# Routing constants later on GpSimd, one gate difference formed on TensorE, six warm-up products fewer

## The chip, the cores and the metric

The program runs on one core of a Trainium2 chip. A core has five engines that run their own instruction streams in order: TensorE (PE, with its weight loads shown as PEld), VectorE (DVE), ScalarE (ACT), GpSimd (POOL) and SyncE (SP), which here issues nearly all transfers. The metric is the device time of one execution in microseconds; lower is better.

## The reference

Three stages follow one another on 1536 tokens (2 batches, 8 heads, 768 steps, 40 columns a head, so 320 columns a token).

```
m_new = np.maximum(f_gate[:, :, t] + m, i_gate[:, :, t])
f_stab = np.exp(f_gate[:, :, t] + m - m_new)
i_stab = np.exp(i_gate[:, :, t] - m_new)
C = f_stab * C + i_stab * outer(v, k);  n = f_stab * n + i_stab * k
y[:, :, t] = sigmoid(o_gate) * (C q) / max(|n q|, 1)
...
h = x @ w_in;  g = softplus(h);  x = g @ w_out            # 320 -> 2048 -> 320
...
e_idx = np.argmax(x @ w_gate, axis=1)                      # one of 8 experts for each token
ye = np.maximum(x[mask] @ w1[e], 0.0) @ w2[e]              # 320 -> 1024 -> 320
out[mask] = gate_w * eom * ye
```

## The kernel before

The steps of the first stage are taken in six chunks of 128, for both batches, as products of 128x128 blocks. The names in the trace are those of the tiles. The gates of a chunk are prepared by `gates`: a scan gives `mm` (the running maximum m), `fg` becomes the decay, its cumulative sum is `acum`, and `ig` becomes i - m. Both `acum` and `ig` are turned by TensorE into one PSUM tile `gps`, and ScalarE takes their exponentials into `gts`. `gates` runs three times: for chunk 0, chunk 1, and chunks 2 to 5 together. Then, for a chunk and a batch: `sp` = k·q, `abc` = the decay between steps (for chunks 2 to 5 it is loaded from DRAM as a broadcast of `acum`, masked by an affine_select on GpSimd, and put through exponentials on ScalarE), `abc<-sp,abc` on VectorE, `pv` = scores times values, `qc` = carried state times q, and `kv`, the update of the carried state `cst`. `kv` reads `v<-v,sm`, which GpSimd makes. The output goes through `y`, is turned (`xp`), and split into a high part `win<-xp` and a low part `wou<-xp`.

The second stage's weights come in packed as `wra` in 16 pieces (a ring of three buffers). Each is converted by three VectorE instructions (`wta<-wra`), cast into a high part (`win<-wta` or `wou<-wta`, 128x704), and the low parts are subtractions: 128x576 on VectorE and 64x128 on GpSimd (function `low_p`). A round of `ph` (eight products) is one of the 16 pieces for one block of 256 tokens; there are 96 rounds. ScalarE makes `ab` of `ph` (three passes), VectorE makes `g`, ScalarE casts it to `gh`, VectorE subtracts for `gl`, and `acc` (six products) reads `gh` and `gl`.

The third stage first routes tokens. `constants` makes what routing needs: fifteen small GpSimd instructions (`tri`, `iota8`, `tokid`, `pad` and others), four loads of the gate weights `wg`, and 19 transfers that clear `rows` in DRAM from `pad`.

The order on the engines is made when the program is built. Each function is a task that yields the engine that it wants next ("P", "A", "V", "G", "S"); a planner (`Weaver`) with a price for each instruction picks the task that could start first by its own clocks, and by rank where they tie. A task that yields a number waits until so many rounds of `ph` have been planned. What is planned is fixed: each engine then runs its stream in order, and waits for semaphores. So a changed task changes the order of many others around it.

`heat` stands first on TensorE: products of a tile of ones that depend on no data. `W.clock["P"]` behind it tells the planner when TensorE is free.

Of the kernel before, what the change touches and what calls it, by code (L numbers as in the profile page):

```python
# [8 lines left out]
F32 = mybir.dt.float32  # L9
F32R = mybir.dt.float32r  # L10
BF16 = mybir.dt.bfloat16
# [3 lines left out]
ALU = mybir.AluOpType  # L15
# [4 lines left out]
RAWS = (2, 3, 3, 3, 3)  # L20
DRAM = bass.MemoryType.DRAM

HEAT = 50
EARLY = 4
P = 128
NEG = -1.0e30
# [208 lines left out]
def mlstm_moe_kernel(ctx: ExitStack, tc: tile.TileContext, q_t, k_t, k, v, i_gate, f_gate, o_gate,  # L235
                     w_in, w_gate, w_og, w1, w2, out):
    nc = tc.nc
    W = Weaver()
    PE, ACT, DVE, POOL, SP = (Priced(W, e, l) for e, l in
                              ((nc.tensor, "P"), (nc.scalar, "A"), (nc.vector, "V"), (nc.gpsimd, "G"), (nc.sync, "S")))  # L240
# [18 lines left out]
    NSP = 2  # L259
# [5 lines left out]
    G = B * H  # L265
# [11 lines left out]
    moe = moe_cm.__enter__()  # L277
# [28 lines left out]
    ig = moe.tile([GG, S], F32, tag="xl0", name="ig")  # L306
    mm = moe.tile([GG, S], F32, tag="row0", name="mm")
# [20 lines left out]
    def events(n, users=1):  # L328
# [15 lines left out]
    ident = const.tile([P, P], F32, name="ident")  # L344
    make_identity(nc, ident)
    identb = const.tile([P, P], BF16, name="identb")
    POOL.tensor_copy(out=identb, in_=ident)
    scratch_all = moe.tile([P, (3 + NSP) * P + P // 2], F32, tag="row2", name="scratch")
    after_t = scratch_all[:, (3 + NSP) * P:].bitcast(BF16)
    POOL.memset(after_t, 0.0)  # L350
    POOL.affine_select(out=after_t, in_=after_t, pattern=[[1, P]], compare_op=ALU.is_ge, fill=NEG, base=0,
                       channel_multiplier=-1)
    scratch = scratch_all[0:GG, 0:(3 + NSP) * P]
# [28 lines left out]
    def heat():  # L382
        warm, ev = yield from bank.get([P, 2 * P], F32, "heat")
        W.clock["P"] = 1.1
        yield "P"
        for _ in range(HEAT):
            PE.matmul(warm, ones, ones.unsqueeze(1).to_broadcast([P, 2, P]), start=True, stop=True)
        W.clock["P"] = 8.1
        W.signal(ev)

    def gates(n, c0, c1):
        yield [have_fi]
        t0, t1 = c0 * P, c1 * P
        p0 = max(t0, 1)
        if n:
            yield [gate_scan[n - 1], have_g[n - 1]]
        yield "V"
        DVE.tensor_tensor_scan(out=mm[:, t0:t1], data0=fg[:, t0:t1], data1=ig[:, t0:t1],
                               initial=NEG if n == 0 else mm[:, t0 - 1:t0], op0=ALU.add, op1=ALU.max)
        if n < 2:  # L400
            W.signal(gate_scan[n])
        yield "V"
        DVE.tensor_tensor(out=fg[:, p0:t1], in0=fg[:, p0:t1], in1=mm[:, p0 - 1:t1 - 1], op=ALU.add)
        yield "V"
        DVE.tensor_tensor(out=fg[:, p0:t1], in0=fg[:, p0:t1], in1=mm[:, p0:t1], op=ALU.subtract)
        yield "V"
        DVE.tensor_scalar(out=fg[:, p0:t1], in0=fg[:, p0:t1], scalar1=-104.0, scalar2=None, op0=ALU.max)
        if n == 0:
            DVE.memset(fg[:, 0:1], 0.0)
        yield "V"  # L410
        for c in range(c0, c1):
            cs = slice(c * P, (c + 1) * P)
            DVE.tensor_tensor_scan(out=acum[:, cs], data0=keep, data1=fg[:, cs], initial=0.0,
                                   op0=ALU.mult, op1=ALU.add)
        have_cum = Event(W.cur.out)
        for c in range(c0, min(c1, NSP)):
            a, p3 = acum[:, c * P:(c + 1) * P], parts3[:, c * P:(c + 1) * P]
            yield "V"
            DVE.tensor_copy(out=p3, in_=a)
            yield "V"  # L420
            DVE.tensor_tensor(out=rest, in0=a, in1=p3, op=ALU.subtract)
            yield "V"
            DVE.tensor_copy(out=p3[32:64], in_=rest[32:64])
            DVE.tensor_copy(out=second[64:GG], in_=rest[64:GG])
            yield "V"
            DVE.tensor_tensor(out=p3[64:GG], in0=rest[64:GG], in1=second[64:GG], op=ALU.subtract)
            have_acum[c].t = W.cur.out
        W.add(store_a(max(c0, NSP), c1, have_cum), 0)
        yield "V"
        DVE.tensor_tensor(out=ig[:, t0:t1], in0=ig[:, t0:t1], in1=mm[:, t0:t1], op=ALU.subtract)  # L430
        gps, gev = yield from bank.get([P, 2, NCH, G], F32, "gps")
        yield "P"
        for c in range(c0, c1):
            PE.transpose(gps[:, 0, c, :], acum[0:G, c * P:(c + 1) * P], ident[:G, :G])
            PE.transpose(gps[:, 1, c, :], ig[0:G, c * P:(c + 1) * P], ident[:G, :G])
        cs = slice(c0, c1)
        yield "A"
        ACT.activation(out=eB[:, cs], in_=gps[:, 1, cs], func=AF.Exp)
        ACT.activation(out=eA[:, cs], in_=gps[:, 0, cs], func=AF.Exp)
        yield "V"  # L440
        DVE.tensor_scalar(out=nA[:, cs], in0=gps[:, 0, cs], scalar1=-1.0, scalar2=None, op0=ALU.mult)
        W.signal(gev)
        for c in range(c0, c1):
            W.signal(have_g[c])
        W.signal(have_gates)
        W.signal(read_acum)
        W.signal(read_parts)
# [3 lines left out]
    def store_a(c0, c1, ready):  # L451
        if c1 <= c0:
            return
        yield [ready, sent_w]
        yield "S"
        SP.dma_start(abc_dram[:, c0 * P:c1 * P], acum[0:G, c0 * P:c1 * P])
        have_ab = Event(W.cur.out)
        yield from loads_a(c0, c1, have_ab)
# [374 lines left out]
    base = const.tile([P, E], F32, name="base")  # L833
# [4 lines left out]
    have_const, have_rows = Event(), Event()  # L838

    def constants():  # L840
        yield 2.0
        yield "G"
        POOL.memset(tri, 1.0)
        POOL.affine_select(out=tri, in_=tri, pattern=[[1, P]], compare_op=ALU.is_gt, fill=0.0,
                           base=0, channel_multiplier=-1)
        POOL.iota(iota8, pattern=[[1, E]], base=0, channel_multiplier=0, allow_small_or_imprecise_dtypes=True)
        POOL.iota(tokid, pattern=[[P, NCH], [S, B]], base=0, channel_multiplier=1, allow_small_or_imprecise_dtypes=True)
        POOL.memset(pad, 0.0)
        POOL.memset(wg[64:P, 2], 0.0)
        POOL.memset(pad[:, CCOL + 1:CCOL + 2], BIG)  # L850
        for t in (room, nxt, s128, esl, base, newp, more_p):
            POOL.memset(t, 0.0)
        POOL.iota(rem, pattern=[[0, 1]], base=0, channel_multiplier=1, allow_small_or_imprecise_dtypes=True)
        yield "S"
        for j, w in enumerate((w_gate, w_og)):
            SP.dma_start(wg[:, 0:2, j * E:(j + 1) * E], w[0:256].rearrange("(a p) e -> p a e", p=P))
            SP.dma_start(wg[0:64, 2, j * E:(j + 1) * E], w[256:DM])
        W.signal(have_const)
        yield 12.0
        for s in range(SLOTS):  # L860
            yield "S"
            SP.dma_start(rows[s * P:(s + 1) * P, :], pad)
        W.signal(have_rows)
# [545 lines left out]
    def low_w2(qn, e, r, ev):  # L1409
# [3 lines left out]
        W.signal(w2_ready[qn])  # L1413

    W.add(heat(), 0)
    W.add(load_gates(), 0)
    W.add(early_a(), 0)
    W.add(gates(0, 0, 1), 0)
    W.add(gates(1, 1, 2), 0.5)
    W.add(gates(2, 2, NCH), 1)  # L1420
    W.add(loads(0, 1), 1)
    W.add(load_w(), 2)
# [4 lines left out]
    for c in range(NCH):  # L1427
        for b in range(B):
            W.add(chunk(b, c), 0 if c == 0 else 1.5 if c == 1 else 2 + 0.1 * c)
    W.add(constants(), 5)  # L1430
    up_t, down_t = Task(up1(), 2.0), Task(down1(), 2.0)
    W.tasks += [down_t, up_t]
# [226 lines left out]
    if SLOTS > NS:  # L1659
        used = nc.values_load(meta[0:1, P:P + 1], min_val=0, max_val=SLOTS * P)  # L1660
        with tc.tile_pool(name="rest", bufs=1) as xp_, tc.tile_pool(name="ps3", bufs=2, space=PSUM) as ps3, \
                ExitStack() as deeper:
            for s in range(NS, SLOTS):
# [32 lines left out]
                for j in range(F // P):  # L1696
# [4 lines left out]
                    out=out, out_offset=bass.IndirectOffsetOnAxis(ap=tkr, axis=0), in_=yr, in_offset=None,  # L1701
# [72 lines left out]
```

## Time and profile before

| what | us |
|---|---|
| median of 3 runs | 435.1 (434.52 to 436.67) |
| profiled execution, device time | 435.17 |
| its span in the trace | 433.5 |
| TensorE busy | 410.1 (95% of the span) |
| VectorE busy | 343.5 (79%) |
| ScalarE busy | 302.5 (70%) |
| GpSimd busy | 181.0 (42%) |

The span runs from the first to the last traced instruction; the device time has 1.67 us more around it. Busy shares are means over stretches with different limits.

### The profile page before, as it was taken

How to read it: one execution, taken by the hardware profiler on the slowest of the kernel's cores; microseconds unless marked ns; L12 is line 12 of the kernel's file. 1: busy time of each engine (PE TensorE's matmuls, PEld its weight loads, DVE VectorE, ACT ScalarE, POOL GpSimd, SP SyncE). 2: the span in 40 equal slices, each digit the busy share in tenths (PEclk: the TensorE clock that was granted, in tenths of full speed). 3: DMA queues.
4: the chain of work that ended last, by engine and by line, in shares of the span. 5: the costliest groups of instructions: out<-in, count | busy, mean ns of one | idle time of the engine just before them, and what ended most of it. 6: DMA issues, size and time to landing. Idle time of an engine off the chain costs nothing. (4 is left out here: it accounts for less than half of the span.)

```text
span 433.5 us, 9833 instructions
## 1 busy us (share of the span) xinstructions
PE 410.1 (95%) x3078; PEld 390.5 (90%) x3078; DVE 343.5 (79%) x904; ACT 302.5 (70%) x879; POOL 181.0 (42%) x246
## 2 busy tenths in 40 slices
PE   8877999999899999999999999899999999999994
PEld 6767999999899999999999999767998998998893
DVE  4999798998999999997657675666755898798663
ACT  2776699996868877777769669466798666566230
POOL 4256756756120111120201102127676287387654
PEclk9999899999999999999999999989999999999998
DMA  8958789499226412032101100128645636544112
GB/s 263 312 175 247 240 240 300 136 332 297 77 102 252 170 69 67 33 91 62 38 2 38 38 2 37 38 102 271 228 132 185 220 132 216 189 144 139 42 67 80
DMA packets 32284, 62.90 MB, mean 145 GB/s; under 512 B 4218, under 2 KB 16765, under 8 KB 32230
## 3 DMA queue, kind: packets, MB, share of 16 engines
q1 hardware_dynamic: 30742, 57.87, 41.0%
q0 software_dynamic: 1488, 4.35, 2.7%
q8 instruction: 28, 0.46, 0.4%
q14 instruction: 26, 0.21, 0.2%
HBM read 54.05 MB, written 8.65 MB: 145 GB/s over the span
## 5 line engine op out<-in xcount | busy, mean ns | idle before, releaser
L196 ACT ACTIVATE ab<-ab 128x256 f32<-128x256 f32 x192 | 77.4, 416 | 2.8
L196 PE MATMUL ph<-w1s,flat 128*128 x312 | 58.8, 332 | 2.6 <-DVE hr L196 1.5
L196 POOL TENSOR_TENSOR w1s<-w1raw,w1s 64x256 fp32r<-64x256 f32 (+1 forms) x39 | 39.4, 1027 | 48.5 <-ACT w1s L196 25.0
L196 PE MATMUL acc<-win,gh 128*128 128x320 f32 x240 | 56.1, 320 | 0.0
L196 DVE SCALAR_TENSOR_TENSOR g<-ph,ab 128x256 f32<-128x256 f32 x96 | 39.9, 419 | 20.2 <-ACT ab L196 19.5
L196 PE MATMUL yp<-w2s,hh 128*128 x240 | 54.6, 315 | 1.0 <-POOL w2s L196 0.9
L196 ACT ACTIVATE ab<-ph 128x256 f32<-128x256 f32 x96 | 36.0, 379 | 26.4 <-PE ph L196 26.2
L196 PEld LDWEIGHTS ph<-w1s,flat 128*128 128x128 f32 x312 | 46.6, 189 | 7.9 <-DVE hr L196 1.9
L196 DVE TENSOR_TENSOR gl<-g,gh 128x256 fp32r<-128x256 f32 x96 | 42.5, 447 | 7.9 <-ACT gh L196 7.2
L196 POOL DMA_INDIRECT rows<-row,rsm x12 | 12.0, 1004 | 80.4 <-DVE rsm L196 47.6
L196 POOL TENSOR_TENSOR w2s<-w2raw,w2s 128x640 fp32r<-128x640 f32 x22 | 39.1, 1808 | 8.7 <-issue 4.9
L196 ACT CAST gh<-g 128x256 fp32r<-128x256 f32 x96 | 38.1, 398 | 6.6 <-DVE g L196 4.7
L196 PEld LDWEIGHTS yp<-w2s,hh 128*128 128x128 f32 x240 | 39.8, 188 | 3.1 <-POOL w2s L196 1.1
L196 PE MATMUL ph<-win 128*128 128x256 f32 x250 | 40.8, 286 | 0.0
L196 DVE TENSOR_TENSOR hr<-ph,hr 128x256 f32<-128x256 f32 x60 | 24.7, 420 | 20.3 <-ACT hr L196 17.2
L196 PEld LDWEIGHTS acc<-win,gh 128*128 128x128 f32 x240 | 39.4, 191 | 0.0
L196 ACT COPY hr<-ph 128x256 f32<-128x256 f32 x60 | 22.6, 376 | 21.3 <-PE ph L196 19.2
L196 PE MATMUL acc<-win,gl 128*128 128x320 f32 x120 | 37.4, 312 | 0.0
L196 PE MATMUL yp<-w2s,hl 128*128 x120 | 37.2, 310 | 0.0
L196 PEld LDWEIGHTS ph<-win 128*128 128x128 f32 x250 | 34.3, 190 | 0.0
L196 PE MATMUL acc<-wou,gh 128*128 128x320 f32 x144 | 33.1, 315 | 1.2 <-ACT gh L196 1.2
L196 ACT CAST w2s<-w2raw 128x640 fp32r<-128x640 f32 x32 | 22.6, 735 | 13.9 <-PE yp L196 13.9
(209 smaller groups left out, 1070.6 us busy)
## 6 DMA issues: line engine op xcount, KB each, us to landing
w1raw<-in_w_dram SPq DMA_DIRECT2D x32, 384.0 KB, 4.4
wra<-in_w_in_dram SPq DMA_DIRECT2D x16, 704.0 KB, 5.1
w2raw<-in_w_dram SPq DMA_DIRECT2D x32, 320.0 KB, 3.2
abc<-abc_dram SPq DMA_DIRECT2D x4, 1024.0 KB, 7.8
rows<-pad SPq DMA_DIRECT2D x19, 194.0 KB, 4.4
qT<-in_q_t_dram SPq DMA_DIRECT2D x6, 512.0 KB, 4.4
kn<-in_k_dram SPq DMA_DIRECT2D x5, 416.0 KB
vn<-in_v_dram SPq DMA_DIRECT2D x6, 320.0 KB, 5.6
```

What stands on the lines that cost most here:

```text
L196: return fn(*args, **kw)
```

## The change

Four edits. The loop `heat` makes 44 products and not 50, and the planner is told 7.8 and not 8.1 for its end. In `gates` the VectorE subtraction `ig - mm` goes; in its place TensorE accumulates, behind the turned `ig`, a product of `mm` with a 16x16 tile `minus` (-1 on the diagonal), so that `gps` holds i - m. The tile `minus` is made by a memset and an affine_select on GpSimd at the start. `constants` waits for 20 planned rounds of `ph` before the GpSimd part (was 2), and for 26 before the clearing of `rows` (was 12).

```diff
-HEAT = 50
+HEAT = 44
...
-    scratch_all = moe.tile([P, (3 + NSP) * P + P // 2], F32, tag="row2", name="scratch")
-    after_t = scratch_all[:, (3 + NSP) * P:].bitcast(BF16)
+    scratch_all = moe.tile([P, (3 + NSP) * P + P // 2 + G], F32, tag="row2", name="scratch")
+    minus = scratch_all[0:G, (3 + NSP) * P + P // 2:]
+    POOL.memset(minus, 0.0)
+    POOL.affine_select(out=minus, in_=minus, pattern=[[-1, G]], compare_op=ALU.not_equal, fill=-1.0, base=0,
+                       channel_multiplier=1)
+    after_t = scratch_all[:, (3 + NSP) * P:(3 + NSP) * P + P // 2].bitcast(BF16)
...
-        W.clock["P"] = 8.1
+        W.clock["P"] = 7.8
...
-        yield "V"
-        DVE.tensor_tensor(out=ig[:, t0:t1], in0=ig[:, t0:t1], in1=mm[:, t0:t1], op=ALU.subtract)
...
-            PE.transpose(gps[:, 1, c, :], ig[0:G, c * P:(c + 1) * P], ident[:G, :G])
+            PE.matmul(gps[:, 1, c, :], ig[0:G, c * P:(c + 1) * P], ident[:G, :G], start=True, stop=False, is_transpose=True)
+            PE.matmul(gps[:, 1, c, :], mm[0:G, c * P:(c + 1) * P], minus, start=False, stop=True)
...
     def constants():
-        yield 2.0
+        yield 20.0
         yield "G"
...
-        yield 12.0
+        yield 26.0
         for s in range(SLOTS):
             yield "S"
             SP.dma_start(rows[s * P:(s + 1) * P, :], pad)
```

The change moves much more than these lines, since the planner runs anew. From the last routing step on, the order on all engines is the same as before (on TensorE the last 1581 rows of the program's order).

**GpSimd, at the update of chunk 1.** Before, with `v_575` the operand of `kv` for batch 1, in front of it the constants, in front of these `cst` of the same update:

```order
L196 TENSOR_TENSOR cst_111<-cst_111,sm 40x4x41 x2
L196 MEMSET tri 128x128
L196 AFFINE_SELECT tri<-tri 128x128
L196 IOTA iota_115 128x8
L196 IOTA tokid 128x12
L196 MEMSET pad 128x388
...
L196 IOTA rem 128x1
L196 TENSOR_TENSOR v_575<-v_378,sm 128x328
L196 TENSOR_TENSOR win<-wta,win 64x128
L196 AFFINE_SELECT abc<-abc 128x4x128
```

Now, where `v_584` is the same operand:

```order
L196 TENSOR_TENSOR cst_115<-cst_115,sm 40x4x41 x2
L196 TENSOR_TENSOR win<-wta,win 64x128
L196 TENSOR_TENSOR v_584<-v_374,sm 128x328
L196 AFFINE_SELECT abc<-abc 128x4x128 x2
L196 TENSOR_TENSOR v_608<-vn_83,gts 128x8x40
```

The constants are gone from here, and the low part of a weight piece stands ahead of the operand, where it stood behind.

**TensorE, behind the first two rounds of `ph`.** Before (`acc_560` and `acc_561` are the first sums of block 0):

```order
L196 MATMUL ph<-wou,win 128x256 x3
L196 MATMUL pv<-v_378,abc 128x123 x6
L196 MATMUL pv<-v_378,abc 128x82
L196 MATMUL pv<-v_378,abc 128x41
L196 MATMUL kv<-v_575,kn_85 104x82 x4
L196 MATMUL acc_560<-win,gh 128x320 x2
```

Now:

```order
L196 MATMUL ph<-wou,win 128x256 x3
L196 MATMUL kv<-v_584,kn_85 104x82 x4
L196 MATMUL sp<-qT_81,kT 128x128 x4
L196 MATMUL acc_569<-win,gh 128x320 x2
L196 MATMUL acc_569<-win,gl 128x320
L196 MATMUL acc_570<-win,gh 128x320 x2
L196 MATMUL acc_570<-win,gl 128x320
L196 MATMUL pv<-v_374,abc 128x123 x6
```

`kv` now follows `ph` at once, one `sp` of chunk 2 stands ahead of the first `acc`, and `pv` behind it.

**ScalarE, at the same place.** Before, with `sm<-abc` the first instruction that reads the loaded and masked `abc` of chunk 2:

```order
L196 CAST win<-wta 128x704
L196 ACTIVATE ab<-ph 128x256 x2
L196 ACTIVATE ab<-ab 128x256 x4
L196 CAST gh<-g 128x256
L196 CAST win<-wta 128x704
L196 CAST gh<-g 128x256
L196 ACTIVATE sm<-abc 128x4
```

Now:

```order
L196 CAST win<-wta 128x704
L196 ACTIVATE y<-y 128x320
L196 ACTIVATE ab<-ph 128x256
L196 ACTIVATE ab<-ab 128x256 x2
L196 ACTIVATE ab<-ph 128x256
L196 ACTIVATE ab<-ab 128x256
L196 ACTIVATE sm<-abc 128x4
L196 ACTIVATE abc<-abc,gts 128x128 x2
L196 ACTIVATE ab<-ab 128x256
L196 CAST gh<-g 128x256
```

The read of the loaded `abc`, which stood behind both `gh`, now stands ahead of the first. On SyncE the clearing transfers `rows<-pad`, which stood as 14 and 5 between loads of chunks 4 and 5 (the last load of `og` behind them), now stand as 12 and 7 behind all loads of the first stage.

## Rows read from the trace of the kernel before

**Rows 1.** Busy time by stretch: us, each engine (instructions), granted clock, DMA share, GB/s.
```profile
9.04:37.22 28.18, 23.67 (x211) 21.25 (x211) 27.24 (x54) 19.09 (x74) 11.15 (x17) 1.00 0.72 247
...
60.00:275.00 215.00, 213.00 (x1710) 211.40 (x1709) 181.41 (x526) 170.59 (x527) 55.47 (x82) 1.00 0.34 112
```

**Rows 2.** The same for the products of ones alone (TensorE).
```profile
1.14:6.00 4.86, 4.86 (x23) 1.00 0.83 210
6.00:9.04 3.04, 3.04 (x29) 1.00 1.01 350
```

**Rows 3.** Timeline of the start, all engines: start us, duration us.
```profile
4.28 2.46 SPq L196 DMA_DIRECT2D wra<-in_w_in_dram  x3
...
8.34 0.29 DVE L196 TENSOR_TENSOR ig<-ig,mm 80x128 f32<-80x128 f32 x1
...
9.13 0.21 PE L196 MATMUL gps<-ident,ig 16*128 16x16 f32 x1
...
12.66 0.52 DVE L196 TENSOR_SCALAR wta<-wra 128x704 uint32<-128x704 uint32 x1
```

**Rows 4.** Transfers issued 4.9 to 5.3: KB, median us to landing.
```profile
wra<-in_w_in_dram SPq DMA_DIRECT2D x1, 704.0 KB, 9.6
```

**Rows 5.** Timeline of VectorE, 30 to 75.
```profile
31.24 0.67 DVE L196 TENSOR_TENSOR ig<-ig,mm 80x512 f32<-80x512 f32 x1
...
37.45 0.87 DVE L196 SCALAR_TENSOR_TENSOR wta<-wra,wta 128x704 uint32<-128x704 uint32 x1
```

**Rows 6.** Timeline of TensorE, 29 to 60; in brackets idle time before, and what ended it.
```profile
37.22 0.84 PE L196 MATMUL ph<-win 128*128 128x256 f32 x5
...
39.21 1.87 PE L196 MATMUL pv<-v,abc 128*128 128x123 f32 x16
43.26 1.47 PE L196 MATMUL kv<-v,kn 128*104 128x82 f32 x8 [2.17 <-POOL v L196]
...
54.91 1.16 PE L196 MATMUL sp<-qT,kT 104*128 104x128 f32 x8 [1.11 <-DVE abc L196]
```

**Rows 7.** Busy time by stretch, columns as in rows 1.
```profile
28.96:31.37 2.41, 0.52 (x4) 0.31 (x4) 2.41 (x5) 2.07 (x8) 1.34 (x3) 1.00 0.01 1
43.00:44.00 1.00, 0.74 (x6) 0.75 (x6) 1.00 (x2) 0.34 (x2) 0.85 (x3) 0.76 0.98 363
44.00:47.00 3.00, 3.00 (x16) 3.00 (x15) 2.84 (x9) 2.23 (x9) 2.53 (x5) 0.51 1.05 344
```

**Rows 8.** Timeline of GpSimd, 39 to 44.
```profile
39.27 0.66 POOL L196 MEMSET tri<- 128x128 bf16 x1
...
42.46 0.74 POOL L196 TENSOR_TENSOR v<-v,sm 128x328 f32<-128x328 f32 x1
43.28 0.58 POOL L196 TENSOR_TENSOR win<-wta,win 64x128 fp32r<-64x128 f32 x1
43.94 0.70 POOL L196 TENSOR_SCALAR_AFFINE_SELECT abc<-abc 128x512 f32<-128x512 f32 x1
```

**Rows 9.** Timeline of ScalarE, 38 to 47.
```profile
38.73 0.77 ACT L196 CAST win<-wta 128x704 fp32r<-128x704 f32 x1
...
41.46 0.41 ACT L196 CAST gh<-g 128x256 fp32r<-128x256 f32 x1 [0.19 <-DVE g L196]
...
44.91 1.28 ACT L196 ACTIVATE abc<-abc,gts 128x128 f32<-128x128 f32 x4
```

**Rows 10.** Timeline of SyncE's issues, 10 to 140.
```profile
34.36 0.39 SPq L196 DMA_DIRECT2D abc<-abc_dram  x1
...
90.18 8.79 SPq L196 DMA_DIRECT2D rows<-pad  x14
```

**Rows 11.** Transfers issued 34 to 34.7: KB, median us to landing.
```profile
abc<-abc_dram SPq DMA_DIRECT2D x1, 1024.0 KB, 8.2
```

**Rows 12.** Timeline, all engines, 103 to 117.
```profile
107.65 0.47 ACT L196 ACTIVATE y<-og 128x320 f32<-128x320 f32 x1 [1.36 <-DMA og<-in_o_gate_dram]
...
109.59 0.71 PE L196 MATMUL sp<-qT,kT 104*128 104x128 f32 x4 [0.55 <-DVE cst L196]
```

## Prediction, made before the changed kernel ran

> **What bounds the kernel now.** I read the busy time by stretch first. TensorE is the bound for most of the run: from 60 to 275 us it is busy 213.0 of 215 us [rows 1]. Whatever makes that stretch begin earlier shortens the run by as much, and whatever loads the other engines there costs nothing until TensorE waits. Ahead of it the picture is another. Between the products of ones and the first `ph` (9.04 to 37.22) TensorE is busy 23.67 of 28.18 us and VectorE 27.24 [rows 1]: VectorE runs without a gap, so work taken from it there comes off the time. Next I read the timeline of TensorE for its waits. The longest in the whole run is 2.17 us ahead of `kv` at 43.26, released by GpSimd's `v` [rows 6]. Behind it the granted clock falls: 0.76 from 43 to 44 and 0.51 from 44 to 47, the lower of its two levels (1.2 against 2.4 GHz), and 1.00 on either side [rows 7]. The time that this costs is 0.24 + 3 x 0.49 = 1.7 us, at the most, since the first row begins in the wait. So one place has cost 3.9 us. GpSimd's timeline says why it is late: `v` ran at 42.46, behind the constants that began at 39.27 [rows 8]. One more wait is near, 1.11 us ahead of `sp` at 54.91 [rows 6].
>
> **The change part by part.**
>
> *Six products of ones.* Their pace is not even: 23 in the first 4.86 us, 29 in the last 3.04 us [rows 2] (0.21 and 0.105 us each), though the granted clock reads 1.00 in both. The six come off the fast end: 0.63 us, so that `gps` can start at 8.4 and not at 9.04.
>
> *The subtraction on VectorE.* Three instructions go: 0.29 us for chunk 0 [rows 3], as much for chunk 1 (the same shape), 0.67 us for chunks 2 to 5 [rows 5]. The six products that replace them cost 0.21 us or less each [rows 3], overlap their neighbours, and stand in stretches in which TensorE has spare time (4.5 us of 28.18 [rows 1]): nothing. If that cover were gone they would cost at most 6 x 0.21 = 1.3 us. The two instructions for `minus` come on GpSimd at the start, which the trace doesn't show in this size; the nearest row is a memset of 128x128 with 0.66 us beside other work [rows 8], so 0 to 1.3 us, and I take nothing, since GpSimd's next operand waits for later loads.
>
> *What the earlier start is worth.* VectorE would reach its first conversion instruction 0.9 us earlier (0.29 + 0.63). It can't start it: three `wra` are issued in 2.46 us from 4.28 [rows 3], so the second at about 5.1, and that one lands 9.6 us later [rows 4], at 14.7. At the 350 GB/s of that stretch [rows 2] 704 KB take 2.1 us, so the first lands at about 12.6. Before, the instruction ran at 12.66 [rows 3]. The head start is spent waiting there, and nothing is left of it. Of the subtractions the two later ones remain, 0.28 + 0.67 = 0.95 us in a gapless stretch. So the first `ph` starts **1.0 us earlier**, at 36.2. Lower bound 0.6 (the order of VectorE's conversions is new, too), upper 1.9 (the load lands early enough after all).
>
> *The constants.* Now the place of the 2.17 us wait, followed in the new order. Two rounds of `ph` take 2.0 us (37.22 to 39.21 [rows 6]) and end at 38.2. `kv` stands next and needs `v`, which GpSimd runs behind `win`, and that waits for ScalarE's cast of the third weight piece. The conversion ended at 38.32 (37.45 + 0.87 [rows 5]), 1.0 earlier is 37.3; cast 0.77 [rows 9], `win` 0.58, `v` 0.74 [rows 8]: 39.4. **TensorE waits 1.2 us.** Then `kv` and one `sp`: half of 1.47 us (that row lies in the low clock) and 0.9 of 1.16 [rows 6], to 41.0. `acc` needs `gh`, and ScalarE now makes `gh` behind its first read of the masked `abc`. That load was issued at 34.36 [rows 10], gated by VectorE's `y`; the subtractions and one `wou` no longer stand ahead of this `y`, so some 1.5 us earlier, at 32.9. It took 8.2 us [rows 11]: landed at 41.1. GpSimd's mask 0.70 [rows 8], then on ScalarE a small read (0.2), two of four exponentials (half of 1.28), one `ab` (0.4, as `gh`) and `gh` 0.41 [rows 9]: 43.5. **TensorE waits 2.5 us more.** So the waits here are 3.7 us where they were 2.17 + 1.11 = 3.3; the later 1.11 I take as gone, since `sp` has eight heads in a row there now and the product on VectorE that frees its bank stands ahead. The waits give back −0.4 us; the constants' 3.2 us are off the path, but a load takes their place.
>
> What decides is the clock. If it stays high, 1.7 us come back. In the trace a wait of 2.17 us in one piece was followed by the low clock; a stretch of 2.41 us with only 0.52 us of work, in two waits, was not: its clock stayed 1.00 [rows 7]. The new waits are in two pieces with 1.6 us of work between them, which is nearer to the second, so I take the clock as high: **+1.7 − 0.4 = 1.3 us**. Both ends stay in the range. The Trainium skill (TensorE: Matmul & The Clock Gate, "HAM oscillation — how this bites in real kernels") says that a matmul stream broken by waits restarts at the lower rate and pays for it each time. The trace shows both, a wait with that end and two without it. By the rule the sum would lose the 1.7 us: that is the second case below.
>
> *The constants and the clearing, where they go.* The constants land at a place where GpSimd is idle three quarters of the time (55.47 us busy of 215 [rows 1]): nothing, or at worst their 3.2 us once more. The 14 clearing transfers stood at 90.18 for 8.79 us [rows 10] ahead of loads that the first stage wants. ScalarE then waited 1.36 us for `og`, and TensorE 0.55 us at 109.59 [rows 12], for a VectorE product behind ScalarE's chain. Now no load of that stage is behind them: **0.55 us**. At least 0; at most 1.4, if all of ScalarE's wait came through.
>
> **Sum:** 1.0 + 1.3 + 0.55 = 2.85 us off 435.17, the time of the profiled execution: **432.3 us**. The median, 435.1, is as good as the same. Behind the last routing step the order is unchanged, so nothing is gained or lost there.
>
> **The rivals.**
> B, *the clock falls again*: the wait of 2.5 us is longer than the 2.17 that was followed by the low clock. It costs 1.7 us: 434.0.
> C, *the waits close*: the first weight piece lands early (0.9 us more), and the load of `abc` too, so that only a third of the 3.7 us is left (2.5 more); with the 0.55 the sum is 6.2 us: 429.0. For it: 4.5 us of TensorE's idle time lie ahead of 37 us. Against: both loads are placed by rows.
> D, *slower*: ScalarE's stream waits in order. `ab`, `gh`, the next casts and with them `acc` are behind the read of `abc`; each us that the load lands behind 41.1 costs one, and the clock is then low. It ends on the slow side from a landing 1.2 us later (42.3), and by over 0.5% from 44.4: 437.3. For it: before, it landed at 42.56. Against: it is issued earlier.
> E, *nothing comes of it*: the planner puts 270 us anew, and waits come in the full stretch (2.0 us of them were there [rows 1]; as many more suffice with B's clock): 435 to 436.
>
> **How the numbers follow.** This kernel's runs spread by 0.5% (434.52 to 436.67), so about 0.5%, 2.2 us, is what can be told from no change: faster means below 432.9. Forecast 0.46, B 0.22, C 0.13, D 0.11, E 0.08. Faster: 0.38 of the forecast (its 0.6 to 1.9 and 0 to 1.4 leave some of it above), 0.13 of C, 0.03 of B: 0.54. Slower: 0.09 of D and 0.01 of E: 0.10. The rest, 0.36, is within. The range reaches into C and up through B and E: 429.8 to 435.6; the forecast's own is 431.2 to 433.2.
>
> **What would show it.** Right: `gps` at about 8.4; VectorE idle until about 12.6 at the first `wta`; first `ph` at 36.2; no constants on GpSimd between `cst` and `v`; TensorE waiting for `kv` about 1.2 us and for the first `acc` about 2.5 us, the latter with ScalarE idle for GpSimd's masked `abc`; granted clock 1.00 from 40 to 50; no wait for `og` at 107. Wrong: a first `ph` later than 36.6, a granted clock of 0.5 behind the wait, or more than 2 us of TensorE's idle time between 60 and 275.

## The result, and the profile after

| | before | after |
|---|---|---|
| median of 8 runs each | 434.98 us (434.52 to 436.67) | 431.15 us (430.29 to 433.17) |
| ratio | | 0.9914, 95% interval 0.9893 to 0.9936 |
| profiled execution | 435.17 us, span 433.5, clock 0.987 | 431.56 us, span 429.9, clock 0.993 |

The change makes the kernel 0.9% faster; the forecast was 432.3 us. Ratios, here and below, leave out executions over 1.5% above the fastest of their kernel (three of 81 of before, one each of all_same and const_gate), while medians and differences of means keep them; without them only the difference of all_same would move by more than 0.15 us, to −3.4. The sum came out by other amounts than its terms, though. Three moments of TensorE, which both orders have in common, divide the run: the first `ph`, the last wait ahead of the routing (`x2tp`, 0.36 us), and the end.

| | first `ph` | from there to `x2tp` | from there to the end |
|---|---|---|---|
| before | 37.22 | 245.69 | 150.59 |
| after | 37.88 (+0.66) | 242.16 (−3.53) | 149.86 (−0.73) |

The first part is longer, where the forecast had it 1.0 us shorter. Busy time by stretch of the kernel after (us, then each engine with its instructions, granted clock, DMA share, GB/s):

```profile
8.95:37.88 28.93, 26.02 (x223) 24.09 (x223) 25.25 (x53) 19.72 (x76) 13.37 (x17) 0.94 0.83 274
60.00:275.00 215.00, 213.94 (x1709) 211.32 (x1709) 181.19 (x543) 167.68 (x524) 59.22 (x96) 1.00 0.35 111
28.88:29.42 0.54, 0.00 (x0) 0.00 (x0) 0.54 (x2) 0.51 (x3) 0.54 (x1) 1.00 0.00 0
29.42:30.91 1.49, 1.49 (x17) 1.46 (x17) 1.49 (x4) 1.27 (x5) 0.23 (x2) 1.00 0.13 33
31.00:34.00 3.00, 3.00 (x15) 3.00 (x16) 1.89 (x4) 0.94 (x4) 3.00 (x2) 0.50 0.65 195
34.00:35.00 1.00, 1.00 (x9) 1.00 (x9) 0.49 (x2) 0.24 (x1) 0.32 (x1) 0.79 0.91 332
37.00:60.00 23.00, 21.36 (x175) 20.54 (x176) 21.18 (x49) 20.87 (x65) 12.67 (x21) 1.00 0.83 245
40.00:50.00 10.00, 8.36 (x66) 7.76 (x66) 8.55 (x21) 9.43 (x32) 6.54 (x11) 1.00 0.64 218
50.00:60.00 10.00, 10.00 (x88) 9.95 (x87) 9.63 (x23) 8.47 (x27) 4.75 (x8) 1.00 0.95 268
```

One stretch of the kernel before, to set beside its like:

```profile
37.00:60.00 23.00, 19.71 (x155) 19.41 (x153) 20.14 (x44) 18.80 (x60) 15.99 (x35) 0.93 0.92 267
```

Against [rows 1], TensorE is busy 2.35 us longer ahead of the first `ph`, and VectorE 2 us less: VectorE waits there now. The granted clock is at its lower level from 31 to 34 us, with 0.79 behind it, which costs 3 x 0.50 + 0.21 = 1.7 us. It fell behind 0.54 us of idle time and 1.49 us of small products in which TensorE counts as busy. At 40 to 50 us, where it was low before [rows 7], it is 1.00. The timeline of TensorE at these places (start us, duration us; in brackets the idle time before, and what ended it):

```profile
29.42 0.23 PE L196 MATMUL gps<-ident,acum 16*128 16x16 f32 x1 [0.54 <-ACT abc L196]
29.51 0.21 PE L196 MATMUL gps<-ident,ig 16*128 16x16 f32 x1
29.57 0.37 PE L196 MATMUL gps<-scratch,mm 16*128 16x16 f32 x2
...
30.91 3.56 PE L196 MATMUL pv<-v,abc 128*128 128x123 f32 x16
...
37.88 0.83 PE L196 MATMUL ph<-win 128*128 128x256 f32 x5
...
41.41 0.96 PE L196 MATMUL kv<-v,kn 128*104 128x82 f32 x8 [1.38 <-POOL v L196]
42.20 1.10 PE L196 MATMUL sp<-qT,kT 104*128 104x128 f32 x8
43.56 0.57 PE L196 MATMUL acc<-win,gh 128*128 128x320 f32 x2 [0.26 <-ACT gh L196]
```

The product of 16 `pv` takes 3.56 us at the low clock. The wait for `v` is 1.38 us where it was 2.17 [rows 6], and the wait for `gh`, forecast at 2.5, is 0.26. The wait of 1.11 us ahead of `sp` [rows 6] is gone: from 50 to 60 us TensorE is busy all the time. VectorE, GpSimd, ScalarE and SyncE of the kernel after:

```profile
12.54 0.50 DVE L196 TENSOR_SCALAR wta<-wra 128x704 uint32<-128x704 uint32 x1
...
38.17 1.00 POOL L196 TENSOR_TENSOR cst<-cst,sm 40x164 f32<-40x164 f32 x2 [3.85 <-PE qc L196]
39.55 0.46 POOL L196 TENSOR_TENSOR win<-wta,win 64x128 fp32r<-64x128 f32 x1 [0.37 <-ACT win L196]
40.09 1.27 POOL L196 TENSOR_TENSOR v<-v,sm 128x328 f32<-128x328 f32 x1
41.31 1.87 POOL L196 TENSOR_SCALAR_AFFINE_SELECT abc<-abc 128x512 f32<-128x512 f32 x2
...
38.70 0.77 ACT L196 CAST win<-wta 128x704 fp32r<-128x704 f32 x1
...
41.97 0.21 ACT L196 ACTIVATE sm<-abc 128x4 f32<-128x4 f32 x1 [0.25 <-POOL abc L196]
...
43.12 0.39 ACT L196 CAST gh<-g 128x256 fp32r<-128x256 f32 x1
...
31.97 0.39 SPq L196 DMA_DIRECT2D abc<-abc_dram  x1
...
134.55 5.51 SPq L196 DMA_DIRECT2D rows<-pad  x8
```

`v` stands behind `cst` and `win` alone. The load of `abc` is issued at 31.97, 2.4 us earlier than before [rows 10] (forecast: 1.5), and the mask follows `v` without waiting for it. ScalarE is held up 0.25 us, for GpSimd's mask and not for the load. The clearing transfers are at 134.55, and no wait for `og` is left at 107 [rows 12].

### The profile page after: what moved, and what is told of

Read it like the earlier page. It is cut to its first block, busy times and chain, and to the rows that moved or that the text cites. A ratio compares the mean times of both kernels' runs of the same rounds, so it can differ in the third digit from the quotient of the medians.

```text
span 429.9 us, 9844 instructions
## 1 busy us (share of the span) xinstructions
PE 410.4 (95%) x3084; PEld 390.1 (91%) x3084; DVE 339.0 (79%) x901; ACT 301.2 (70%) x879; POOL 182.4 (42%) x248
## 5 line engine op out<-in xcount | busy, mean ns | idle before, releaser
L196 POOL TENSOR_TENSOR w1s<-w1raw,w1s 64x256 fp32r<-64x256 f32 (+1 forms) x39 | 40.9, 1063 | 44.4 <-ACT w1s L196 23.9
L196 DVE TENSOR_TENSOR gl<-g,gh 128x256 fp32r<-128x256 f32 x96 | 41.6, 440 | 8.2 <-ACT gh L196 7.0
L196 ACT CAST gh<-g 128x256 fp32r<-128x256 f32 x96 | 38.1, 398 | 6.1 <-DVE g L196 4.9
```

The source lines that it names most:

```text
L196: return fn(*args, **kw)
```

## The experiments

Executions of one kernel differ by how long the clock was low, so each has, beside its time, its **lost clock time**: (1 − mean granted clock) x span. Over 81 executions of the kernel before, on three chips, the time rises by 0.72 us for each us lost. Of the lost time 0.8 to 2.2 us lie behind the last product in the fourteen profiles, where TensorE has nothing left to do. Ten executions lost under 2 us; their mean is 432.7 us. Thirty-nine lost over 4.6 us; theirs is 436.5. So the table gives, beside the ratio, the difference of the means of (time − 0.7 x lost clock time), "at equal clock", with an interval got by drawing the executions again. Kernels of one group ran on one chip with their own runs of before.

| kernel | median (executions), us | before, us | ratio, 95% | at equal clock, us |
|---|---|---|---|---|
| only_heat | 434.00 (12) | 436.17 | 0.9951 [0.9916, 0.9986] | −0.7 [−1.3, −0.1] |
| const_start | 434.15 (12) | 436.17 | 0.9974 [0.9938, 1.001] | −0.3 [−1.0, 0.3] |
| clear_late | 433.36 (10) | 436.17 | 0.9933 [0.99, 0.9967] | −1.8 [−2.5, −1.1] |
| gate_same | 434.67 (12) | 436.17 | 0.9976 [0.9947, 1.0006] | −0.7 [−1.4, 0.1] |
| after_again | 431.93 (11) | 435.15 | 0.992 [0.9889, 0.9951] | −2.4 [−3.0, −1.8] |
| warm_after | 432.55 (9) | 435.15 | 0.9933 [0.9903, 0.9964] | −1.5 [−2.1, −1.0] |
| all_same | 430.88 (6) | 435.15 | 0.9885 [0.9844, 0.9926] | −3.0 [−4.3, −1.7] |
| only_const | 435.02 (12) | 435.15 | 0.9999 [0.9973, 1.0025] | +0.7 [0.2, 1.2] |
| all_again | 431.89 (5) | 436.5 | 0.988 [0.983, 0.9929] | −3.2 [−3.7, −2.7] |
| const_gate | 435.05 (12) | 436.5 | 0.9962 [0.993, 0.9994] | −0.7 [−1.4, 0.0] |
| all_50 | 432.23 (7) | 436.5 | 0.9923 [0.9885, 0.996] | −2.8 [−3.4, −2.2] |
| all_warm | 431.79 (9) | 436.5 | 0.9926 [0.9886, 0.9967] | −3.0 [−3.6, −2.4] |

**Each part alone, in before's order.** The order of the instructions is kept by leaving the planner's prices as they were and giving the moved instructions out elsewhere.

*only_heat*

```diff
-HEAT = 50
+HEAT = 44
-        W.clock["P"] = 8.1
+        W.clock["P"] = 7.8
```

> The kernel before with 44 products of ones for 50 and nothing else; the order on every engine is that of before. Theory (the six products are worth nothing, since the next stage waits for the first piece of the weight, and the products run slowly until the clock has risen): gps starts 0.1 to 0.6 us earlier, the first conversion instruction on VectorE at 12.6 as before, time within 0.3 us of before. Rival (the head start is real): 0.6 us faster.

Nearer to the rival: −0.7 us at equal clock, with an interval (0.1 to 1.3) that does not rule the theory out (the medians are 2.2 us apart, but these hold more of the clock). The first conversion instruction on VectorE, in the kernel with 44:

```profile
8.58 0.23 PE L196 MATMUL gps<-ident,acum 16*128 16x16 f32 x1
...
12.74 0.76 DVE L196 TENSOR_SCALAR wta<-wra 128x704 uint32<-128x704 uint32 x1 [0.26 <-DMA wra<-in_w_in_dram]
```

Here it waits for the load. In [rows 3] its row has no bracket: it did not wait for the load, but came out of VectorE's own chain, 3.62 us behind `gps`. Two other profiles with 50 products (gate_same, const_gate) have `gps` at 9.31 and 9.46 and `wta` at 13.15 and 13.30, again with no wait; where `wta` waited for the load, it began between 12.04 (after_again, all_warm) and 12.74, and in all_same at 11.80 without a wait. So the load lands between 11.8 or earlier and 12.7, VectorE is ready 3.6 us or more after `gps`, and the later one counts. In the profiles the products end between 7.4 and 9.5 us, as TensorE speeds up sooner or later; six products fewer help where that is late.

*const_start* (the planner still prices the constants where they stood, but GpSimd runs them ahead of everything)

```diff
+    def make_constants(G_):
+        G_.memset(tri, 1.0)
...
+    make_constants(nc.gpsimd)
```

> The kernel before with the constants made by GpSimd ahead of everything else, in before's order of all other instructions. Theory (the constants' place at 39 to 43 us and the low clock behind that wait are worth most of the gain): the wait for v at kv falls from 2.17 us to under 0.6, the granted clock stays 1.00 from 40 to 50 us, and the run is 2.0 to 3.5 us faster. Rival 1 (the gain is the clearing transfers and the full stretch): under 0.8 us faster. Rival 2 (the low clock only moves to another wait or stretch): the wait goes, but another 2 to 3 us of low clock appears before 60 us, and the run is at most 1 us faster.

The theory fails: 0.3 us at equal clock. In its profile the wait at `kv` is gone, but the low clock lies at 31 to 41 us instead (the row below), so that the first `ph` came at 41.01 with all its operands ready.

```profile
31.00:41.00 10.00, 9.73 (x51) 9.48 (x52) 6.35 (x13) 2.55 (x9) 1.43 (x1) 0.53 0.69 206
```

The profile is rival 2's. But a lost clock alone would not show at equal clock, and 5 of the 12 executions lost over 4.6 us, no more than before's 15 of 33 on that chip; 0.3 us fits rival 1 (under 0.8) as well. Two things that the traces show make the wait worth less than its 2.17 us. Where the clock falls ahead of the first `ph`, the wait for `v` is short even with the constants in their old place: 0.62 us in only_heat (clock low at 30 to 34 us, the first row below), 0.71 in gate_same. And the load of `og`, behind the clearing transfers, takes back part of what is saved: ScalarE's wait for it, 1.36 us in [rows 12], is 1.88 here, and TensorE's behind it 1.07, where it was 0.55 (the other two rows).

```profile
42.34 0.96 PE L196 MATMUL kv<-v,kn 128*104 128x82 f32 x8 [0.62 <-POOL v L196]
...
109.00 0.47 ACT L199 ACTIVATE y<-og 128x320 f32<-128x320 f32 x1 [1.88 <-DMA og<-in_o_gate_dram]
...
110.95 0.71 PE L199 MATMUL sp<-qT,kT 104*128 104x128 f32 x4 [1.07 <-DVE cst L199]
```

How much of the 2.17 us each of the two takes is not shown.

*clear_late*

```diff
-            SP.dma_start(rows[s * P:(s + 1) * P, :], pad)
...
+        yield 26.0
+        for s in range(SLOTS):
+            nc.sync.dma_start(rows[s * P:(s + 1) * P, :], pad)
```

> The kernel before with the 19 clearing transfers behind the first stage's loads, nothing else; every other engine's order is before's. Theory: the wait for og at 107 us goes, TensorE's wait of 0.55 us at 109.59 with it, 0.3 to 0.6 us faster. Rival 1: 1.0 to 1.4 us faster (all of ScalarE's wait came through, and the full stretch owes its 1 us to it). Rival 2: nothing, the wait only moves.

Rival 1. The kernel repeats before's waits up to 54.62 us (before 54.91 [rows 6]), and both `sp` waits at 109 and 112 us are gone. What comes next:

```profile
54.62 1.16 PE L199 MATMUL sp<-qT,kT 104*128 104x128 f32 x8 [1.11 <-DVE abc L199]
113.28 1.15 PE L199 MATMUL pv<-v,abc 128*128 128x123 f32 x8 [0.60 <-DVE num L199]
```

Before, this `pv` began at 115.02. That is 1.74 us, less the 0.29 it was early already: 1.45 us. `x2tp` shows as much: 245.69 us behind the first `ph` before, 244.33 here. TensorE's busy time between these two instructions, before and with the clearing late (us, busy, instructions, clock):

```profile
54.91:115.02 60.11, 58.56 (x493) 1.00 0.76 233
```

```profile
54.62:113.28 58.66, 58.06 (x493) 1.00 0.57 175
```

Idle time shrinks from 1.55 to 0.60 us: the 0.55 of [rows 12] and 0.41 more, 2 us behind it. The same 493 instructions also take 0.50 us less. All of that lies behind the first of the two waits (4.43 us busy from 109.59 to 115.02 before, 3.93 from 108.75 to 113.28 here, with the DMA queues all but idle in both), so here a wait in the stream costs more than its idle time.

*gate_same*

```diff
-        DVE.tensor_tensor(out=ig[:, t0:t1], in0=ig[:, t0:t1], in1=mm[:, t0:t1], op=ALU.subtract)
...
+            nc.tensor.matmul(gps[:, 1, c, :], mm[0:G, c * P:(c + 1) * P], minus, start=False, stop=True)
```

> The kernel before with the gate difference formed by TensorE and the subtraction on VectorE gone, every other instruction in before's order. Theory (VectorE runs without a gap up to 37 us, so what leaves it comes off): first ph 0.6 to 1.0 us earlier, the wait for v at kv longer by as much where the constants still stand, since GpSimd's constants begin when its queue is free; 0.3 to 1.0 us faster. Rival 1 (nothing is left of it, since the wait for v takes it): within 0.3 us. Rival 2 (twelve small products ahead of pv bring the low clock at 31 us, as in the changed kernel): granted clock near 0.5 from 31 to 34 us, first ph as late as before or later, no gain.

0.7 us at equal clock, with an interval that just holds nothing. The profile is rival 2's, a little later: the clock was at 0.50 from 34 to 40 us, and the first `ph` came at 41.02.

```profile
34.00:40.00 6.00, 6.00 (x32) 5.96 (x31) 2.19 (x5) 0.47 (x3) 0.92 (x1) 0.50 1.06 308
```

**The kernel after again, with products of ones, and the order.**

*after_again* is the changed kernel itself.

> The changed kernel once more, on the chip of the next three, so that more executions and their clocks stand beside those of before. Theory (the gain has two parts, about 2.2 us that every execution shows and 2.2 us of low clock that only falls in fewer of them): executions that lose under 2 us to the low clock are at 430.0 to 430.8, against 432.6 of before; most others lie 1 to 1.5 us above; none or few lose over 4.6 us. Rival (the gain is the clock alone): executions with under 2 us lost are within 0.7 us of those of before.

No execution lost under 2 us here; with the eight of the first comparison two of 19 did, at 430.3 and 430.5 us, 2.3 below before's mean. One of 19 lost over 4.6 us, against 39 of 81 of before (12 of 25 on this chip). So both parts of the gain are there: some 2.4 us at equal clock, and the rest by fewer executions that lose much. The forecast for most others (1 to 1.5 us above) was wrong: they spread from 430.2 to 434.5 us.

*warm_after*

```diff
+            for _ in range(2 if n == 2 else 0):
+                nc.tensor.matmul(gpt[:, 256:512], ones, ones.unsqueeze(1).to_broadcast([P, 2, P]), start=True, stop=True)
...
+                for _ in range(16 if (b, c, p) == (1, 1, 0) else 0):
+                    nc.tensor.matmul(kvt[:, 384:512], ones, ones, start=True, stop=True)
```

> The changed kernel with 8 products of ones (256 columns) set among the four triples of gps for chunks 2 to 5, and 16 of 128 columns ahead of the kv that waits for v at 40 us; all else in the order of the changed kernel. Theory (the clock falls behind TensorE's idle time and the tiny products of gps, and costs 1.7 us there): granted clock 1.00 from 30 to 36 us, pv in 1.9 us where it took 3.56, the run 0.7 to 1.7 us faster than the changed kernel. Rival 1 (the fall has nothing to do with what stands there): the clock is 0.5 from 31 to 34 as before, and the 0.8 us of added products make the run 0.3 to 0.8 us slower. Rival 2 (the time saved is lost again in the wait for v): clock 1.00, first ph 1.5 us earlier, but the wait for v longer by as much, within 0.4 us.

Its timeline of TensorE:

```profile
28.94 0.38 PE L438 MATMUL gps<-ones 128*128 128x256 bf16 x2 [0.55 <-ACT abc L196]
...
32.01 1.98 PE L196 MATMUL pv<-v,abc 128*128 128x123 f32 x16
```

Its busy time in the stretch (columns as above):

```profile
30.00:36.00 6.00, 6.00 (x54) 5.49 (x54) 4.06 (x8) 2.11 (x8) 2.74 (x2) 1.00 0.80 248
```

The clock stayed at 1.00 and `pv` took 1.98 us, as the theory had it. But from the first small product or product of ones to `pv` it now takes 3.07 us, where 29.42 to 30.91 is 1.49: the eight products cost 1.6 us, not 0.8. The first `ph` is at 37.35, in after_again at 37.02 with the low clock. The kernel is 0.9 us slower than after_again at equal clock (interval 0.2 to 1.5). The added products cost as much as the low clock did.

*only_const*

```diff
     def constants():
-        yield 2.0
+        yield 20.0
...
-        yield 12.0
+        yield 26.0
```

> The kernel before with the constants and the clearing moved alone, and the order worked out anew by the planner; VectorE's subtraction and the 50 products of ones stay. Theory (the clearing is worth 1.2 to 1.4 us, the constants up to 0.5 us beside what the clock does): 431.0 to 431.6 in executions with little low clock, median 432 to 434. Rival (the gate difference on TensorE is needed for the gain): 432.3 or above in such executions, median 435.

The rival: nothing is left, and at equal clock the kernel is 0.7 us slower than before (const_start and clear_late, the same two parts in before's order, are 0.3 and 1.8 faster). Yet the constants are off the place, the clock is 1.00 from 30 to 50 us, and no wait for `og` is left. The rows of SyncE, GpSimd, ScalarE and TensorE:

```profile
34.34 0.39 SPq L196 DMA_DIRECT2D abc<-abc_dram  x1
...
42.44 1.47 POOL L196 TENSOR_SCALAR_AFFINE_SELECT abc<-abc 128x512 f32<-128x512 f32 x2 [1.02 <-DMA abc<-abc_dram]
...
43.11 0.21 ACT L196 ACTIVATE sm<-abc 128x4 f32<-128x4 f32 x1 [1.53 <-POOL abc L196]
...
40.41 0.96 PE L196 MATMUL kv<-v,kn 128*104 128x82 f32 x8 [1.06 <-POOL v L196]
45.21 0.56 PE L196 MATMUL acc<-win,gh 128*128 128x320 f32 x2 [1.13 <-ACT gh L196]
54.06 0.93 PE L196 MATMUL kv<-v,kn 128*104 128x82 f32 x8 [1.55 <-issue]
```

The load is issued as late as before, ScalarE's stream waits for it in order, and TensorE stands idle 1.06 + 1.13 + 1.55 = 3.74 us, where it waited 2.17 + 1.11. What ended the last of these the profile doesn't show ("issue"). The 0.5 us between the two sums are not all that is lost against clear_late. Among what else is new are waits of 0.84 us ahead of `ph` at 125 us and of 0.91 ahead of `x2tp` (before: 0.36); the rest was not followed. From here to the changed kernel there are only the gate difference and the six products: 3.1 us at equal clock (interval 2.5 to 3.6), on the same chip.

*all_same* and *all_again* (one kernel: the four edits above together)

> All four parts of the change in before's order of the instructions (constants at the start of GpSimd, clearing behind the first stage's loads, gate difference by TensorE, 44 products of ones). Theory (the parts carry the gain, and the new order as such little): executions with little low clock at 430.4 to 431.2, median 432 to 433.5, since the clock can still fall at 31 us. Rival (the replanned order carries it): executions with little low clock at 432 or above, median over 434.

> All four parts in before's order once more (the same kernel as all_same), beside the three below. Theory (the order worked out anew is worth nothing): as fast as the changed kernel or up to 0.7 us faster, median 430.5 to 432.0, and the first ph at 36.2 to 37.0 in a profile whose clock stays 1.00 from 30 to 36. Rival (the six executions of all_same were lucky): median 432.5 or above.

Both rivals fail, and the new order is not needed for the gain. all_same's median of 430.88 us is faster than its theory had it (432 to 433.5), and all_again's of 431.89 is within its own. Against after_again on the same chip it is −0.6 us at equal clock, interval −1.9 to 0.7, which does not tell the two orders apart. The two profiles differ by 5.3 us in the first `ph`, although the kernel is the same:

```profile
29.84 0.52 PE L199 MATMUL xp<-ident,y 128*128 128x128 f32 x3 [1.97 <-POOL cst L199]
...
36.41 0.84 PE L199 MATMUL ph<-win 128*128 128x256 f32 x5
```

That is all_same's timeline of TensorE, and this its busy time by stretch:

```profile
30.00:36.00 6.00, 6.00 (x58) 5.86 (x58) 5.08 (x9) 2.33 (x9) 1.72 (x2) 1.00 0.49 157
```

The same two views of all_again:

```profile
30.43 0.52 PE L199 MATMUL xp<-ident,y 128*128 128x128 f32 x3 [2.60 <-POOL cst L199]
...
41.75 0.84 PE L199 MATMUL ph<-win 128*128 128x256 f32 x5
```

```profile
35.00:40.00 5.00, 5.00 (x27) 4.96 (x27) 1.93 (x4) 0.47 (x3) 0.00 (x0) 0.50 1.10 330
```

With the clock high the first `ph` is 0.81 us earlier than in the profile of before.

*const_gate* (const_start and gate_same together) and *all_50* (all_same with 50 products of ones)

> Constants at the start of GpSimd and gate difference by TensorE in before's order; 50 products of ones; the clearing transfers where they were, at 90 us. Theory (the clearing costs 1.2 to 1.5 us at 107 us, by itself, and adds to the rest): the waits for og and behind it are back, 1.2 to 1.5 us slower than all_50. Rival (once the rest is early, ScalarE has slack for og): within 0.5 us of all_50.

> As all_again with 50 products of ones, not 44. Theory (the head start is spent waiting for the first piece of the weight): within 0.3 us of all_again, the first conversion instruction on VectorE at the same time to 0.2 us. Rival (the head start is real): 0.5 to 0.7 us slower than all_again.

const_gate is 2.1 us slower than all_50 at equal clock (interval 1.3 to 2.9): the theory of the clearing, and above its bounds, though the interval reaches them. The wait is back, on ScalarE:

```profile
108.52 0.47 ACT L199 ACTIVATE y<-og 128x320 f32<-128x320 f32 x1 [1.05 <-DMA og<-in_o_gate_dram]
```

all_50 is 0.4 us slower than all_again, interval −0.2 to 1.0: between theory and rival. In these two profiles the first `wta` came at 12.17 and 12.29, as the theory had it. With only_heat (0.7) it points to about half a us for the six products, which neither interval shows to be more than 0.1.

*all_warm*

```diff
+            for _ in range(14):
+                nc.tensor.matmul(spare[:, 0:P], ones, ones, start=True, stop=True)
```

> As all_again, with 14 products of ones (128 columns each, into a bank that is free) between sp and the xp that TensorE waits for at 28 to 30 us; they fill idle time and hold nothing up. Theory (the clock falls at 30 to 34 us behind that idle time): granted clock 1.00 from 30 to 36 us in the profile, fewer executions with more than 2 us lost to the low clock, 0.5 to 1.5 us faster than all_again. Rival (the fall moves to another place, as with the added products in the changed kernel): within 0.4 us, and low clock at another place.

The timeline of TensorE, and the busy time in the stretch:

```profile
27.95 0.95 PE L759 MATMUL spare<-ones 128*128 128x128 bf16 x14
30.08 0.52 PE L199 MATMUL xp<-ident,y 128*128 128x128 f32 x3 [1.18 <-POOL cst L199]
```

```profile
30.00:36.00 6.00, 5.92 (x56) 5.81 (x57) 5.12 (x10) 2.35 (x9) 1.96 (x2) 1.00 0.46 148
```

The rival, as far as the time goes: +0.2 us against all_again at equal clock, interval −0.4 to 0.7, and the same mean of lost clock time (3.8 us each). The profiled execution kept its clock, but three of nine executions lost over 4.6 us; where in the run they lost it, no trace shows.

## Why the prediction was right, and where it wasn't

The time and its sign were right, in part by luck. In the profile the run is 3.6 us shorter, for a forecast of 2.85: the stretch ahead of the first `ph` missed its term by 1.66 us to the slow side, the stretch from there to `x2tp` its terms (1.3 + 0.55 for 3.53) by 1.68 to the fast side, and the end brought 0.73 that had no term. One of the signs that it named for being wrong, a first `ph` later than 36.6, came true. By its own steps:

- *Six products.* "The head start is spent waiting there" failed. It came of a row that shows no wait: `wta` at 12.66 [rows 3] was taken for the landing of the load, because an estimate of that landing gave the same number. In the kernel after, `wta` at 12.54 did not wait either. The runs give 0.7 and 0.4 us for the six. `gps` at 8.4 failed too, in the profile: it came at 8.95, with 23 products in the first 4.86 us as before, seven in the next 0.90, and 18 in 2.05 (a product that runs across an edge counts on both sides, so that these make 48 for 44, and the 23 and 29 of [rows 2] 52 for 50). The six were taken off the fast end, and in this execution the chip was late to speed up.
- *First `ph` 1.0 us earlier.* In the profile it is 0.66 later; the 1.7 us of low clock at 31 us are as much as the difference. The low clock *ahead* of the first `ph` stood in no rival; B looked for it behind the waits alone. (VectorE, taken as without a gap there, was idle 0.94 of 28.18 us by [rows 1]; after the change it is idle 3.68 of 28.93.) Where the clock stays high, and in before's order, all_same is 0.81 earlier and all_warm 0.57, but clear_late, which changes nothing there, is 0.38 earlier too. So no run with a high clock contradicts the term, but none shows it in the new order by itself. The low clock is not peculiar to that order: six of the ten profiles in before's order have it between 30 and 41 us (the kernel before itself does not).
- *The waits, −0.4.* The first was right (1.38 for 1.2). The second was mis-sized: 0.26 for 2.5. `gh` ended at 43.51, as forecast (43.5). TensorE came to it late: `kv` started at 41.41 and not at 39.4, since ScalarE's cast of the third piece ended at 39.47 and not at 38.1, and `v` took 1.27 us and not 0.74. GpSimd's mask then followed `v`, so a load that landed at the forecast 41.1 would not have been waited for either. Rival C, the load landing early, describes this place only in its result; of rival D, ScalarE held up by the load, nothing is there. What the prediction described is nearer to what only_const does, where mask, ScalarE and TensorE wait for the load in turn; that its idle time sums to 3.74 us for a forecast of 3.7 is chance, for the terms are others (1.06 and 1.13 for 1.2 and 2.5). So in the new order the constants give nothing as long as the load of `abc` comes late. With the gate difference and the six products it is issued 2.4 us earlier; which of these two does it was not run apart. In before's order the gate difference brings it 0.46 us (33.90 in gate_same), and const_gate is no faster than gate_same (−0.7 us each).
- *The clock, +1.7.* At 40 to 50 us it stays at 1.00, as forecast; the loss of the same size at 31 us takes it back. The end gains 0.73 us that no term had. From 286 to 290 us the granted clock was 0.59 before and is 1.00 now, in an order that the change does not touch. It was low between 282 and 292 us in six of the twelve other profiles too. That the clock makes the 0.73 us is not shown: clear_late has it at 1.00 there, and its end takes 150.53 us, as before's 150.59.
- *The clearing, 0.55.* Mis-sized: 1.4 us by clear_late's trace, 1.8 and 2.1 at equal clock in two comparisons. The price was read from one wait of TensorE; the 1.4 of ScalarE's wait, given as the most, was nearer. No other part alone measured as much.

The four parts alone add up to 0.7 + 0.3 + 1.8 + 0.7 = 3.5 us at equal clock, and all of them together in before's order give 3.0 to 3.2. So the gain is theirs, and does not need the new order: the changed kernel, with 2.4, may have lost a bit by it. In the profile 0.94 of the 3.53 us between first `ph` and `x2tp` are less idle time from 60 to 275 us; less idle time and higher clock from 37 to 60 make 1.65 (21.36 busy for 19.71) + 1.6 (0.07 of 23), 0.7 more than is left. That part of the sum stays open: work has changed sides of the first `ph`.

The Trainium skill (TensorE: Matmul & The Clock Gate, "HAM oscillation — how this bites in real kernels") has a broken matmul stream restart at the lower rate. The runs agree that it happens and not that it must: idle 1.85 us ahead of `xp`, only_heat's clock fell; idle 1.97, all_same's did not. What decides between them is not settled here. The changed kernel has fewer executions that lose over 4.6 us (1 of 19 for 39 of 81), but of all_same, all_again, all_50 and all_warm together 7 of 27 have, too few to tell the two orders apart, and which stretch makes the difference is not shown: in both profiles of the changed kernel the clock ahead of `ph` was low from 31 to 35 us at most, in four of before's order for 6 to 10 us, and one profile shows one execution.

## What to carry to other kernels

A row without a bracket did not wait: an estimate that puts a load's landing just there is no evidence that the load was the last to come. A wait of an engine that works in order (ScalarE for `og`, 1.36 us) is better priced at its full length when its chain feeds TensorE, even where TensorE's nearest wait shows less (0.55 here, for 1.4 us or more). And taking one late operand away is worth no more than what is late next allows: look for the load behind it (`abc` in only_const, `og` in const_start), and move that too.

## What was not expected of the hardware

The profile's granted clock reads 1.00 while the products of ones run at half their later pace (23 in 4.86 us, then 18 in 2.05), and the moment of the change differs: 32 of 44 had begun by 6 us in after_again, 23 of 44 in the kernel after. One kernel, all_again, had executions from 430.53 to 435.82 us as its lost clock time went from about 1.3 to 8.7 us; over the kernel before, each us lost cost 0.72 us. Products of ones in idle time (14 in 0.95 us) did not make low clock rarer, as far as nine executions against five can say.
